# Making a positional bias by distance: a first layer over 304 to 576 columns, results read out of PSUM forwards and backwards, rows stored in a skewed raster

## The chip, the cores and the metric

The kernel runs on one core of a Trainium2 chip. The metric is the device time of one execution in microseconds; the time of a kernel is the median of several runs.

## The reference

Attention with a positional bias, followed by two feed-forward stages. The bias is what the change is about:

```
B, H, S, D = 2, 8, 576, 64          # hidden = 32
scores = scale * q @ k^T
rel = pos[:, None] - pos[None, :]
x = log1p(|rel|) / log1p(max(pos_i, 1))          # S x S
h = relu(x * w1 + b1)                            # S x S x 32
bias = h @ w2                                    # S x S x 8, one plane per head
attn = softmax(scores + bias);  out = attn @ v
# then: a mixture of 4 experts (512 -> 1024 -> 512) on 1152 tokens,
# then: a layer 512 -> 2048 -> 512 with a rational function between
```

In a row i the first factor of x depends on the column only by the distance |i - j|; the second is one number for the row.

## The kernel before

**The bias phase.** The 576 rows of the bias are made in 36 groups (`gg`) of 16 rows. Multiplied by the row's log, the hidden layer needs no division: h * psi_i = relu(w1 * log1p(|rel|) + b1 * psi_i). The partitions hold 4 rows x 32 hidden units. `hidden(gg)` makes four tiles of 128 x 576, each an addition of a per-partition shift and a maximum with zero (VectorE) or a Relu with a bias (ScalarE), out of the table `ltab` (1,148 columns: log distances, moved by one column from each of the four rows to the next, so that a window of 576 columns at the right place is what four rows need). `HIDDEN` names the engine of each: three on VectorE ("D"), one on ScalarE ("A"). `products(gg)` multiplies them on TensorE by `wm` (the second layer of the hidden network for 4 rows x 8 heads) into a pair of PSUM banks, half of the columns to a bank; three such pairs rotate. `combine(gg)` evacuates them on ScalarE, times one over the row's log, into the tile `bo`; a tile holds four groups, and two of them rotate (tag `we` of `wpool`, which the expert weights use later). After each fourth group `store` writes the tile to scratch in DRAM (`bias_d`, one tensor per 128 rows), and `load_bias` brings back 128 rows for two heads at a time, with rows on the partitions. The last 64 rows go straight from `bo` into place (`last_bias`) as well.

**Order.** Instructions run on each engine in the order in which they are written. Groups overlap: hidden rows run `LEAD` = 2 groups ahead of the products, evacuations one group behind them; hidden rows have room for four groups. SyncE's queue carries nearly all DMAs, in order: loads of q, k and v, eight small loads of constants (`setup_const`, at group 3), the stores, the loads of the bias, and the swapped copy of k (`swap_k`). Meanwhile GpSimd splits q, k and v into a high and a low part, and TensorE transposes the first of them (`qk_T`). At groups 34 and 35 the first two score groups of the attention are put in (`scores`, `biased` on VectorE, `exps` on ScalarE).

**The attention** follows in an order that a planner (`Flow`) writes out from fixed costs and due times, among them `BIAS4`, the time at which the last band of the bias is taken to be in place. It needs the stacks of q and k, the swapped k, and the bias of its rows, in groups of 128 rows and one head. Then come the expert stage and the last stage, which keep TensorE busy; the diff touches of them only the size of one tile.

Of the kernel before, what the change touches and what calls it, by code (L numbers as in the profile page):

```python
# [9 lines left out]
F32 = mybir.dt.float32  # L10
# [14 lines left out]
P = 128  # L25
# [12 lines left out]
W_MAX = f32_of_bits(0x47EFFFFF - (48 << 23))  # L38


NTQ, NDT = S // 4, 1148
LEAD = 2
START = dict(PE=0.0, ACT=2.1, DVE=2.7, POOL=3.6, SP=5.5)
BIAS4 = 7.6
EARLY_SPLIT = {22: 'k'}
EARLY = {34: (0,), 35: (1,)}
HIDDEN = ["DDDA"] * (S // 16)
OUT_DVE = ()

LAG = {"PE": .2, "ACT": .16, "DVE": .17, "POOL": .14, "SP": 2.2, "": 0.0, "own": .1, "ownPE": 0.0}  # L50
CFG = dict(S=(-46.52, 288.45, 1.92, 183.94), R=(52.57, 7.45, 22.77, 52.37),
# [83 lines left out]
class Kernel:  # L135
# [16 lines left out]
    def run(self):  # L152
# [3 lines left out]
        self.wpool = ctx.enter_context(self.pool("wpool"))  # L156
        self.stacks = ctx.enter_context(self.pool("stacks"))
        self.dram = ctx.enter_context(self.pool("dscr", DRAM))
        self.bias_d = [self.dram.tile([P, H, S] if c < 4 else [16, H, 4, S], F32, name=f"bias_d{c}") for c in range(5)]
        self.nc.scalar.preload_act_table_set("natural_log_exp_and_others")  # L160
        self.ident = self.const.tile([P, P], F32, name="ident")
        self.w_tiles = {}
# [125 lines left out]
    def load_parts(self, i, key, a, b, stg, defer):  # L288
        nc = self.nc
        if key == ("d", 0):  # L290
            hi, lo = (self.up.tile([P, a, b], F32R, tag="w64", bufs=2, name="wd" + x) for x in "hl")
        elif len(key) == 2 or (i - 2 * NPAIR + 1) % 10 < 2:
            w = self.wpool.tile([P, 4 * S], F32R, tag="we", bufs=2, name="we")
            hi, lo = (w[:, o:o + a * b].rearrange("p (a b) -> p a b", a=a) for o in (0, a * b))
        else:
            hi, lo = (self.wmoe.tile([P, a, b], F32R, tag="wm" + x, bufs=8, name="wm" + x) for x in "hl")
        nc.scalar.activation(out=hi, in_=stg, func=AF.Copy)  # L297
        self.w_tiles[key] = (hi, lo)

        def low():  # L300
            for k in range(0, a, a // 2):
                sl = slice(k, k + a // 2)
                nc.gpsimd.tensor_tensor(out=lo[:, sl], in0=stg[:, sl], in1=hi[:, sl].bitcast(F32), op=ALU.subtract)  # L303
            self.stage_w()
        defer(low)
# [65 lines left out]

    def bias_phase(self):
        nc, t, pa = self.nc, self.t, self.pa
        cw = pa.tile([P, 10], F32, name="cw")
        mask = pa.tile([P, 4], F32, name="mask")
        shift = pa.tile([P, NTQ], F32, name="shift")
        rpsi = pa.tile([P, S // 16], F32, name="rpsi")
        ltab = pa.tile([P, NDT], F32, name="ltab")  # L380
        nc.sync.dma_start(out=cw, in_=t["w1_b1_w2"])
        nc.scalar.dma_start(out=shift, in_=t["c_psi"])
        for i, (a, b) in enumerate(((NDT - 640, NDT), (0, NDT - 640))):
            nc.sync.dma_start(out=ltab[:, a:b], in_=t["c_ltab"][:, a:b])
            if i:
                nc.scalar.dma_start(out=rpsi, in_=t["c_rpsi"])
            else:
                nc.scalar.dma_start(out=mask, in_=t["c_mask"])
                nc.scalar.dma_start(out=self.ident, in_=t["c_ident"])
# [1 line left out]
            self.load_raw(0, nm)  # L391
        w1, b1 = cw[:, 0:1], cw[:, 1:2]
        nc.vector.tensor_scalar(out=shift, in0=shift, scalar1=b1, scalar2=None, op0=ALU.mult)
        nc.vector.tensor_scalar(out=ltab[:, NDT - 640:NDT], in0=ltab[:, NDT - 640:NDT], scalar1=w1, scalar2=None, op0=ALU.mult)
        wm = pa.tile([P, 4, H], F32, name="wm")
        nc.gpsimd.tensor_tensor(out=wm, in0=cw[:, 2:10].unsqueeze(1).to_broadcast([P, 4, H]),
                                in1=mask.unsqueeze(2).to_broadcast([P, 4, H]), op=ALU.mult)
        wm = wm.rearrange("p g h -> p (g h)")

        NG = S // 16  # L400
        hid, outs, banks = {}, {}, {}
        hids = self.xpool.tile([P, 16, S], F32, tag="xa", bufs=1, name="hid")

        def hidden(gg):
            for q in range(4):
                if q % 2 == 0:
                    slot = (2 * gg + q // 2) % 8
                ht = hid[gg, q] = hids[:, 2 * slot + q % 2]
                tt = 4 * gg + q
                d, c = ltab[:, 572 - 4 * tt:572 - 4 * tt + S], shift[:, tt:tt + 1]  # L410
                e = HIDDEN[gg][q]
                if e == "A":
                    nc.scalar.activation(out=ht, in_=d, func=AF.Relu, bias=c)  # L413
                else:
                    eng = nc.vector if e == "D" else nc.gpsimd
                    eng.tensor_scalar(out=ht, in0=d, scalar1=c, scalar2=0.0, op0=ALU.add, op1=ALU.max)  # L416


        def products(gg):
            ps = banks[gg] = self.ps.tile([P, 2, 512], F32, tag="ab", bufs=3, name="ps_ab")  # L420
            hs = [hid.pop((gg, q)) for q in range(4)]
            for i in range(2):
                for q in range(4):
                    nc.tensor.matmul(ps[32 * q:32 * q + 32, i, 0:288], lhsT=wm, rhs=hs[q][:, 288 * i:288 * i + 288], start=True, stop=True)  # L424

        def store(b):
            if b < 8:
                d = self.bias_d[b // 2][64 * (b % 2):64 * (b % 2) + 64].rearrange("(a q) h j -> (q h) a j", a=4)
            else:
                d = self.bias_d[4].rearrange("q h a j -> (q h) a j")  # L430
            nc.sync.dma_start(out=d, in_=outs[b])

        def combine(gg):
            b, G = divmod(gg, 4)
            if G == 0:
                outs[b] = self.wpool.tile([P, 4, S], F32, tag="we", bufs=2, name="bo")
            bo, ps = outs[b][:, G].rearrange("p (a b) -> p a b", a=2), banks.pop(gg)[:, :, 0:288]
            c = rpsi[:, gg:gg + 1]
            if gg in OUT_DVE:
                nc.vector.tensor_scalar(out=bo, in0=ps, scalar1=c, scalar2=None, op0=ALU.mult)  # L440
            else:
                nc.scalar.activation(out=bo, in_=ps, func=AF.Copy, scale=c)  # L442
            if G == 3:
                if b == 8:
                    self.bias_t[0, 4] = self.last_bias(outs[b].rearrange("(q h) a j -> h q a j", h=H))
                    self.last_band = lambda: store(b)
                else:
                    store(b)

        for gg in range(LEAD):  # L450
            hidden(gg)
        nc.vector.tensor_scalar(out=ltab[:, 0:NDT - 640], in0=ltab[:, 0:NDT - 640], scalar1=w1, scalar2=None, op0=ALU.mult)
        for nm in "kqv":
            self.split(0, nm)
            self.load_raw(1, nm)
# [25 lines left out]
                    self.swap_k(0)  # L481


    def last_bias(self, d):

        nc = self.nc
# [5 lines left out]
    def load_bias(self, p, c):  # L492
        d = self.bias_d[c]
        if c < 4:
            bt = self.front.tile([P, 2, S], F32, tag=f"bias{c}", bufs=1, name="bias")
            self.nc.sync.dma_start(out=bt, in_=d[:, 2 * p:2 * p + 2])
        else:
            bt = self.last_bias(d[:, 2 * p:2 * p + 2].rearrange("q h a j -> h q a j"))
        self.bias_t[p, c] = bt
# [745 lines left out]
def shape_consts():  # L1245
# [2 lines left out]
    Pp = np.log1p(np.maximum(d, np.float32(1.0)))  # L1248
    g = np.repeat(np.arange(4), 32)
    m = np.arange(NDT)  # L1250
    ltab = L[np.minimum(np.abs(m[None, :] - 572 - g[:, None]), S - 1)]
    r = 4 * np.repeat(np.arange(4), 32) + np.tile(np.repeat(np.arange(4), H), 4)
    rpsi = np.float32(1.0) / Pp[16 * np.arange(S // 16)[None, :] + r[:, None]]
# [2 lines left out]
        "c_mask": 8.0 * (g[:, None] == np.arange(4)[None, :]).astype(np.float32),  # L1256
        "c_psi": np.ascontiguousarray(Pp[4 * np.arange(NTQ)[None, :] + g[:, None]]),
        "c_rpsi": np.ascontiguousarray(rpsi),
        "c_ltab": np.ascontiguousarray(ltab),
    }  # L1260

# [22 lines left out]
```

## Time and profile before

| | |
|---|---|
| median of 3 runs | 808.4 us (808.29 to 808.88) |
| profiled execution: its time | 807.95 us |
| its span, first to last instruction | 806.0 us |
| TensorE / VectorE / ScalarE / GpSimd busy in the span | 97% / 81% / 61% / 56% |
| granted clock of TensorE | 0.999 |

The profile is of one execution. A row of a timeline has the start, the time until the last end, the engine and line, and what was written from what, merged over instructions of the same kind that follow each other; in square brackets stands idle time before it and what ended it. In rows that group instructions, busy time and mean duration stand behind the count, then the idle time in front of them. SPq is the queue of SyncE. PE is TensorE, DVE VectorE, ACT ScalarE, POOL GpSimd.

### The profile page before, as it was taken

To read this page: it belongs to the slowest core of one execution; us is meant where nothing else is said; L and a number is where in the kernel's file an instruction comes from. 1 tells how busy PE (TensorE), PEld (TensorE's weight loads), DVE (VectorE), ACT (ScalarE), POOL (GpSimd) and SP (SyncE) were. 2 spreads that over 40 slices of the span, in tenths; PEclk is the share of its full clock that TensorE was granted. 3 is DMA by queue.
4 is the path that set the end of the run, shared out by engine and by line. 5 is a ranking of instruction groups with operands and counts; after the bars stand their busy time and mean duration, and the time that the engine had idled before them with its cause. 6 is when DMAs were issued, how large, how long until landed. Compare 5 with 4: busy or idle time off the path is not lost.

```text
span 806.0 us, 13644 instructions
## 1 busy us (share of the span) xinstructions
PE 783.1 (97%) x4980; PEld 683.0 (85%) x4980; DVE 649.4 (81%) x1183; ACT 488.3 (61%) x932; POOL 455.0 (56%) x454
## 2 busy tenths in 40 slices
PE   6888999999999999999999999999999999999997
PEld 2337899988998999999999999999889889998986
DVE  7987888888687888878889878888678667888775
ACT  5898898889443334333333433333369998887772
POOL 3167689778346555444355545345166977754442
PEclk9999999999999999999999999999999999999999
DMA  5788747491013434432444333333130311000012
GB/s 127 264 284 229 196 104 201 105 233 54 1 30 102 131 131 129 137 116 93 147 139 144 131 105 119 117 131 105 40 105 27 119 64 53 1 0 1 1 40 78
DMA packets 67634, 87.37 MB, mean 108 GB/s; under 512 B 33520, under 2 KB 42096, under 8 KB 67440
## 3 DMA queue, kind: packets, MB, share of 16 engines
q1 hardware_dynamic: 66992, 86.35, 35.4%
q8 instruction: 39, 0.64, 0.3%
q14 instruction: 27, 0.22, 0.1%
q10 hardware_dynamic: 576, 0.16, 0.1%
HBM read 60.12 MB, written 21.36 MB: 101 GB/s over the span
## 4 chain that ended last, share of the span: by engine, by line
PE 77%; ACT 7%; POOL 6%; issue 4%; DVE 4%; DMA 2%; SPq 0%; POOLq 0%; DVEq 0%; ACTq 0%
PE ps_o L900 20%; PE ps_o L1150 11%; PE ps_y L992 10%; PE ps_h L1142 10%; PE ps_x L992 8%; PE ps L701 6%; PE ps L594 5%; PE ps L653 4%; ACT hid L413 2%; ACT bo L442 2%; POOL we L303 2%; PE ps_x L890 1%; PE ps L548 1%; POOL wml L303 1%; PE ps_y L890 1%
## 5 line engine op out<-in xcount | busy, mean ns | idle before, releaser
L900 PE MATMUL ps_o<-we,hs 128*128 128x512 f32 x810 | 203.4, 392 | 0.0
L900 PEld LDWEIGHTS ps_o<-we,hs 128*128 128x128 f32 x810 | 146.1, 188 | 25.8
L303 POOL TENSOR_TENSOR we<-wstg,we 128x512 fp32r<-128x512 f32 x40 | 57.0, 1446 | 130.3 <-ACT we L297 130.3
L906 DVE SCALAR_TENSOR_TENSOR acc<-ps_o,prob,acc 128x512 f32<-128x512 f32 x135 | 99.7, 743 | 30.1 <-PE ps_o L900 29.9
L1123 POOL TENSOR_TENSOR qq<-qq,ha 128x384 f32<-128x384 f32 x48 | 48.9, 1019 | 71.0 <-ACT qq L1120 71.0
L1150 PE MATMUL ps_o<-wmh,hs 128*128 128x512 f32 x252 | 83.5, 392 | 1.1 <-POOL hs L1134 1.1
L1142 PE MATMUL ps_h<-x,wmh 128*128 128x384 f32 x288 | 73.7, 337 | 0.0
L636 POOL TENSOR_SCALAR P<-P,ri 128x576 f32<-128x576 f32 x72 | 53.0, 747 | 33.3 <-DVE ri L627 18.8
L930 ACT ACTIVATE hs<-ps_x 128x576 fp32r<-128x576 f32 x32 | 20.8, 651 | 80.7 <-DVE ps_x L1004 74.0
L608 DVE CUSTOM_DVE_ANT_0 P<-ps,bias 128x576 f32<-128x576 f32 x72 | 53.6, 750 | 14.9 <-PE ps L594 12.9
L424 PE MATMUL ps_ab<-hid,wm 128*32 128x288 f32 x576 | 47.0, 425 | 12.0 <-DVE hid L416 7.5
L616 ACT ACTIVATE P<-P,nm 128x576 f32<-128x576 f32 x72 | 56.0, 780 | 3.3 <-DVE nm L608 3.1
L1129 DVE SCALAR_TENSOR_TENSOR qq<-qq,rr 128x384 f32<-128x384 f32 x48 | 26.6, 554 | 38.1 <-ACT rr L1128 35.1
L1150 PEld LDWEIGHTS ps_o<-wmh,hs 128*128 128x128 f32 x252 | 47.3, 188 | 11.4 <-POOL hs L1134 1.9
L328 POOL TENSOR_TENSOR wu<-wt,wu 128x512 fp32r<-128x512 f32 x28 | 36.2, 1314 | 36.4 <-ACT wu L324 36.4
L1142 PEld LDWEIGHTS ps_h<-x,wmh 128*128 128x128 f32 x288 | 52.6, 188 | 2.0
L682 DVE TENSOR_TENSOR ptl<-ps,pth 128x512 fp32r<-128x512 f32 x72 | 48.5, 683 | 5.2 <-ACT pth L678 4.7
L416 DVE TENSOR_SCALAR hid<-ltab,shift 128x576 f32<-128x576 f32 x108 | 52.6, 558 | 0.0
L594 PE MATMUL ps<-kh,qs 128*128 128x288 f32 x168 | 50.3, 321 | 1.4 <-DVE nm L608 1.3
L1134 POOL TENSOR_TENSOR hs<-pp,hs 128x384 fp32r<-128x384 f32 x48 | 48.9, 1019 | 3.5 <-issue 2.8
L424 PEld LDWEIGHTS ps_ab<-hid,wm 128*32 128x32 f32 x576 | 18.4, 112 | 37.0 <-ACT bo L442 13.9
L1150 PE MATMUL ps_o<-wml,hs 128*128 128x512 f32 x126 | 49.5, 393 | 0.0
(142 smaller groups left out, 2098.9 us busy)
## 6 DMA issues: line engine op xcount, KB each, us to landing
wstg<-moe_w SPq DMA_DIRECT2D x32, 512.0 KB, 3.7
bias_d<-bo SPq DMA_DIRECT2D x9, 1152.0 KB, 5.4
bias<-bias_d SPq DMA_DIRECT2D x16, 576.0 KB, 5.1
w<-moe_w_in SPq DMA_DIRECT2D x16, 512.0 KB, 4.4
w<-moe_w_out SPq DMA_DIRECT2D x16, 512.0 KB, 3.8
kl<-kh SPq DMA_DIRECT2D x16, 288.0 KB, 4.4
w_u<-wmag SPq DMA_DIRECT2D x16, 256.0 KB, 2.4
w_d<-wmag SPq DMA_DIRECT2D x16, 256.0 KB, 2.4
```

Source lines behind the costliest of these rows:

```text
L303: nc.gpsimd.tensor_tensor(out=lo[:, sl], in0=stg[:, sl], in1=hi[:, sl].bitcast(F32), op=ALU.subtract)
L416: eng.tensor_scalar(out=ht, in0=d, scalar1=c, scalar2=0.0, op0=ALU.add, op1=ALU.max)
L424: nc.tensor.matmul(ps[32 * q:32 * q + 32, i, 0:288], lhsT=wm, rhs=hs[q][:, 288 * i:288 * i + 288], start=True, stop=True)
L594: nc.tensor.matmul(ps[:, half, dst:dst + w], lhsT=lhs, rhs=k[:, src:src + w], start=(i == 0), stop=(i == len(m) - 1))
L608: nc.vector.tensor_tensor_reduce(out=Pt[u][:, S * h:S * h + S].rearrange("p (a b) -> p a b", a=2), in0=ps[:, :, 0:288], in1=self.bias_t[n ...
L616: nc.scalar.activation(out=pt, in_=pt, func=AF.Exp, scale=-1.0, bias=stat.pop(g), accum_out=sums[n, c][:, h:h + 1])
L636: nc.gpsimd.tensor_scalar(out=pt[:, sl], in0=pt[:, sl], scalar1=ri, scalar2=1.0, op0=ALU.mult, op1=ALU.mult)
L900: nc.tensor.matmul(ps, lhsT=a, rhs=w[:, f, :], start=(f == i == 0), stop=(f == 1 and i == 2))
L906: nc.vector.scalar_tensor_tensor(out=acc[:, t], in0=ps, scalar=pr, in1=acc[:, t], op0=ALU.mult, op1=ALU.add)
L992: nc.tensor.matmul(ps[:, half, 0:288], lhsT=wu[:, w, i, k], rhs=x[v][:, k, 288 * half:288 * half + 288], start=(start and k == j == 0), st ...
L1142: nc.tensor.matmul(ps, lhsT=w[:, k, fo:fo + P], rhs=v[:, k, :], start=(k == i == 0), stop=(k == 3 and i == 2))
L1150: nc.tensor.matmul(ps, lhsT=a[:, P * tt:P * tt + P], rhs=w[:, f % 2, :], start=(f == i == 0), stop=(f == 3 and i == 2))
```

## The change

The first 32 groups no longer make all 576 columns of their rows. They make the hidden layer once for each distance that occurs in the group, from 0 to the largest: 576 - 16 gg or 16 gg + 16 columns, whichever is more (304 to 576). The table for it, `dtab`, has 576 columns. The last four groups work as before, from the 640 columns of `ltab` that they need. A product of up to 512 columns is one matmul per tile and lies in one bank. `combine` reads it twice on ScalarE: once backwards, for the columns left of the diagonal, and once forwards; both write into one row of 591 columns. That row is the same raster for all rows of the group, though each row should be shifted by one column against the next; the shift is made in DRAM, where rows are stored at a pitch of 608 elements, and groups 16 elements closer, so that `load_bias` can read row q one element earlier than its pitch says. A tile of evacuated rows now holds two groups, and each group is stored by itself. The last four groups go into place in twelve loads instead of three. Of each three groups, two have all four hidden tiles on VectorE and one has three.

```diff
-NTQ, NDT = S // 4, 1148
+NTQ, NDT = S // 4, 640
+ROW = 608
+MARGIN = 15
...
-HIDDEN = ["DDDA"] * (S // 16)
-OUT_DVE = ()
+HIDDEN = ["DDDD", "DDDD", "DDDA"] * (S // 48)
...
-        self.bias_d = [self.dram.tile([P, H, S] if c < 4 else [16, H, 4, S], F32, name=f"bias_d{c}") for c in range(5)]
+        self.bias_d = [self.dram.tile([P + 1, H * ROW] if c < 4 else [16, H, 4, S], F32, name=f"bias_d{c}") for c in range(5)]
...
-            w = self.wpool.tile([P, 4 * S], F32R, tag="we", bufs=2, name="we")
+            w = self.wpool.tile([P, 2048], F32R, tag="we", bufs=2, name="we")
...
+        dtab = pa.tile([P, S], F32, name="dtab")
...
-        for i, (a, b) in enumerate(((NDT - 640, NDT), (0, NDT - 640))):
-            nc.sync.dma_start(out=ltab[:, a:b], in_=t["c_ltab"][:, a:b])
+        for i, (tab, nm) in enumerate(((dtab, "c_dtab"), (ltab, "c_ltab"))):
+            nc.sync.dma_start(out=tab, in_=t[nm])
...
-        nc.vector.tensor_scalar(out=ltab[:, NDT - 640:NDT], in0=ltab[:, NDT - 640:NDT], scalar1=w1, scalar2=None, op0=ALU.mult)
+        nc.vector.tensor_scalar(out=dtab, in0=dtab, scalar1=w1, scalar2=None, op0=ALU.mult)
...
+        NM = 32
...
+        def width(gg):
+            return max(S - 16 * gg, 16 * gg + 16) if gg < NM else S
...
-                ht = hid[gg, q] = hids[:, 2 * slot + q % 2]
+                ht = hid[gg, q] = hids[:, 2 * slot + q % 2, 0:width(gg)]
...
-                d, c = ltab[:, 572 - 4 * tt:572 - 4 * tt + S], shift[:, tt:tt + 1]
+                d, c = dtab[:, 0:width(gg)] if gg < NM else ltab[:, 572 - 4 * tt:572 - 4 * tt + S], shift[:, tt:tt + 1]
...
+            W = width(gg)
+            for i, (a, b) in enumerate(((0, min(W, 512)), (512, W)) if gg < NM else ((0, 288), (288, W))):
+                if b > a:
+                    for q in range(4):
+                        nc.tensor.matmul(ps[32 * q:32 * q + 32, i, 0:b - a], lhsT=wm, rhs=hs[q][:, a:b], start=True, stop=True)
+
+        def store(gg):
+
+            b, G = divmod(gg, 2)
+            o = (P * ROW - 16) * (gg % 8)
+            d = self.bias_d[gg // 8].rearrange("q x -> (q x)")[o:o + P * ROW].rearrange("(p r) -> p r", r=ROW)
+            nc.sync.dma_start(out=d[:, 0:S + MARGIN], in_=outs[b][:, G])
+
+        def store_last():
             for i in range(2):
-                for q in range(4):
-                    nc.tensor.matmul(ps[32 * q:32 * q + 32, i, 0:288], lhsT=wm, rhs=hs[q][:, 288 * i:288 * i + 288], start=True, stop=True)
-
-        def store(b):
...
+                nc.sync.dma_start(out=self.bias_d[4].rearrange("q h a j -> (q h) a j")[:, 2 * i:2 * i + 2], in_=outs[16 + i])
 
         def combine(gg):
-            b, G = divmod(gg, 4)
+            b, G = divmod(gg, 2)
+            c = rpsi[:, gg:gg + 1]
+            if gg < NM:
+                if G == 0:
+                    outs[b] = self.wpool.tile([P, 2, S + MARGIN], F32, tag="we", bufs=2, name="bo")
+                ps = banks.pop(gg).rearrange("p a s -> p (a s)")
+                m = 16 * gg + MARGIN
+                nc.scalar.activation(out=outs[b][:, G, 0:m], in_=ps[:, 1:m + 1][:, ::-1], func=AF.Copy, scale=c)
+                nc.scalar.activation(out=outs[b][:, G, m:], in_=ps[:, 0:S - 16 * gg], func=AF.Copy, scale=c)
+                store(gg)
+                return
             if G == 0:
-                outs[b] = self.wpool.tile([P, 4, S], F32, tag="we", bufs=2, name="bo")
+                outs[b] = self.wpool.tile([P, 2, S], F32, tag="we", bufs=2, name="bo")
...
+            if gg == NG - 1:
+                self.last_bias_tile()
+                for i in range(2):
+                    self.last_bias_part(self.bias_t[0, 4], outs[16 + i].rearrange("(q h) a j -> h q a j", h=H), i)
+                self.last_band = store_last
...
-        nc.vector.tensor_scalar(out=ltab[:, 0:NDT - 640], in0=ltab[:, 0:NDT - 640], scalar1=w1, scalar2=None, op0=ALU.mult)
+        nc.vector.tensor_scalar(out=ltab, in0=ltab, scalar1=w1, scalar2=None, op0=ALU.mult)
...
+    def last_bias_part(self, bt, d, i):
+
+        for k in range(2):
+            a, b = (slice(64 * h + 2 * i + k, 64 * h + 64, 4) for h in range(2))
+            for out, src in ((bt[a, 0], d[0, :, k]), (bt[b, 0, 0:512], d[1, :, k, 64:S]), (bt[b, 0, 512:S], d[1, :, k, 0:64])):
+                self.nc.sync.dma_start(out=out, in_=src)
...
-            self.nc.sync.dma_start(out=bt, in_=d[:, 2 * p:2 * p + 2])
+            o = MARGIN + 2 * p * ROW
+            d = d.rearrange("q x -> (q x)")[o:o + P * (H * ROW - 1)].rearrange("(q x) -> q x", q=P)[:, 0:2 * ROW]
+            self.nc.sync.dma_start(out=bt, in_=d.rearrange("q (h r) -> q h r", h=2)[:, :, 0:S])
```

## Rows read from the trace of the kernel before

**Rows 1.** Windows: busy time of each engine, granted clock, DMA share, GB/s.
```profile
45.00:50.00 5.00, 4.38 (x65) 1.69 (x55) 5.00 (x13) 5.00 (x9) 5.00 (x1) 1.00 0.98 333
100.00:110.00 10.00, 9.99 (x79) 9.06 (x77) 9.09 (x27) 9.16 (x23) 8.97 (x13) 1.00 0.53 120
```

**Rows 2.** Forms of instructions, first 66 us.
```profile
L416 DVE TENSOR_SCALAR hid<-ltab,shift 128x576 f32<-128x576 f32 x108 | 52.6, 558 | 0.0
...
L413 ACT ACTIVATE hid<-ltab,shift 128x576 f32<-128x576 f32 x36 | 29.3, 822 | 2.9 <-DVE ltab L394 2.9
L442 ACT ACTIVATE bo<-ps_ab,rpsi 128x576 f32<-128x576 f32 x36 | 28.3, 792 | 7.0 <-PE ps_ab L424 4.3 <-DMA bias_d<-bo 2.6
```

**Rows 3.** Timeline of VectorE, first 30 us.
```profile
4.96 2.67 DVE L416 TENSOR_SCALAR hid<-ltab,shift 128x576 f32<-128x576 f32 x6
...
8.35 9.93 DVE L416 TENSOR_SCALAR hid<-ltab,shift 128x576 f32<-128x576 f32 x13
...
18.20 9.95 DVE L416 TENSOR_SCALAR hid<-ltab,shift 128x576 f32<-128x576 f32 x23
```

**Rows 4.** Timeline of GpSimd: the last split in the early stretch.
```profile
13.03 1.48 POOL L532 TENSOR_TENSOR splv<-rawv,splv 128x576 fp32r<-128x576 f32 x1
```

**Rows 5.** Timeline of all engines, end of the bias phase.
```profile
55.73 2.65 DVE L416 TENSOR_SCALAR hid<-ltab,shift 128x576 f32<-128x576 f32 x6
...
57.35 2.47 PE L424 MATMUL ps_ab<-hid,wm 128*32 128x288 f32 x32 [0.50 <-ACT bo L442]
...
60.47 1.18 PE L424 MATMUL ps_ab<-hid,wm 128*32 128x288 f32 x16
60.58 0.76 DVE L608 CUSTOM_DVE_ANT_0 P<-ps,bias 128x576 f32<-128x576 f32 x1 [2.20 <-PE ps L594]
...
63.99 0.72 ACT L442 ACTIVATE bo<-ps_ab,rpsi 128x576 f32<-128x576 f32 x1
...
64.73 1.85 SPq L489 DMA_DIRECT2D bias<-bo  x3
```

**Rows 6.** Timeline of ScalarE, 33 to 36 us.
```profile
33.26 0.51 ACT L556 ACTIVATE kh<-ps 128x384 fp32r<-128x384 f32 x1
33.63 0.80 ACT L413 ACTIVATE hid<-ltab,shift 128x576 f32<-128x576 f32 x1
34.30 0.77 ACT L442 ACTIVATE bo<-ps_ab,rpsi 128x576 f32<-128x576 f32 x1
34.92 0.81 ACT L413 ACTIVATE hid<-ltab,shift 128x576 f32<-128x576 f32 x1
```

**Rows 7.** Waits from 15 to 62 us: total, times, longest.
```profile
ACT bo L442 <- DMA bias_d<-bo: 2.6, 1, 2.6
```

**Rows 8.** Forms of instructions, whole span.
```profile
L622 DVE TENSOR_SCALAR sm<-sm 128x1 f32<-128x1 f32 x72 | 8.3, 145 | 1.8 <-ACT P L616 1.4
...
L678 ACT ACTIVATE pth<-ps 128x512 fp32r<-128x512 f32 x72 | 41.4, 604 | 4.1 <-PE ps L653 3.5
...
L678 ACT ACTIVATE peh<-ps 128x256 fp32r<-128x256 f32 x16 | 6.3, 394 | 0.0
```

**Rows 9.** Tile wmag: duration in ns, least, median, most; first and last start.
```profile
L361 DVE TENSOR_SCALAR wmag<-wmag x32: 408/418/1400, 259.6 to 562.9; 128x512 uint32<-128x512 uint32 x32
```

**Rows 10.** Timeline of all engines, 67 to 75 us.
```profile
67.77 0.60 SPq L562 DMA_DIRECT2D kl<-kh  x1
...
70.33 0.20 DVE L622 TENSOR_SCALAR sm<-sm 128x1 f32<-128x1 f32 x2
...
74.53 0.38 PE L594 MATMUL ps<-kh,qs 128*128 128x288 f32 x1
```

**Rows 11.** The page's DMA issues: count, KB each, us from issue to landing.
```profile
bias_d<-bo SPq DMA_DIRECT2D x9, 1152.0 KB, 5.4
...
kl<-kh SPq DMA_DIRECT2D x16, 288.0 KB, 4.4
w_u<-wmag SPq DMA_DIRECT2D x16, 256.0 KB, 2.4
```

More of the change, by code (lines that the diff above doesn't have):

```diff
@@ L421, in products @@
             hs = [hid.pop((gg, q)) for q in range(4)]
-            for i in range(2):
-                for q in range(4):
-                    nc.tensor.matmul(ps[32 * q:32 * q + 32, i, 0:288], lhsT=wm, rhs=hs[q][:, 288 * i:288 * i + 288], start=True, stop=True)
-        def store(b):
[L427 to L431, printed above, removed]
@@ L435, in combine @@
             if G == 0:
-                outs[b] = self.wpool.tile([P, 4, S], F32, tag="we", bufs=2, name="bo")
+                outs[b] = self.wpool.tile([P, 2, S], F32, tag="we", bufs=2, name="bo")
             bo, ps = outs[b][:, G].rearrange("p (a b) -> p a b", a=2), banks.pop(gg)[:, :, 0:288]
[L438 to L448, printed above, removed]
+            nc.scalar.activation(out=bo, in_=ps, func=AF.Copy, scale=c)
+            if gg == NG - 1:
[3 more added lines that the diff above has]
+                self.last_band = store_last
@@ L481, in bias_phase, with last_bias_tile @@
                     self.swap_k(0)
+    def last_bias_tile(self):
+        self.bias_t[0, 4] = self.front.tile([P, 2, S], F32, tag="bias4", bufs=1, name="bias")
+    def last_bias_part(self, bt, d, i):
[3 more added lines that the diff above has]
+                self.nc.sync.dma_start(out=out, in_=src)
     def last_bias(self, d):
@@ L1250, in shape_consts @@
     m = np.arange(NDT)
+    dtab = np.broadcast_to(L[None, :], (P, S))
     ltab = L[np.minimum(np.abs(m[None, :] - 572 - g[:, None]), S - 1)]
@@ L1258, in shape_consts @@
         "c_rpsi": np.ascontiguousarray(rpsi),
+        "c_dtab": np.ascontiguousarray(dtab),
         "c_ltab": np.ascontiguousarray(ltab),
```

## The prediction

> **What bounds the kernel now.** I first cut the span into windows and compared the stretch in which the bias is made with a later one. In the later stretch TensorE is busy all the time. In the bias stretch TensorE has holes, while VectorE, ScalarE and the 16 DMA engines all stand at or near full [rows 1]. So what happens there is decided by a race of three, and the rest of the kernel merely starts when the race is over. The forms of the instructions name the racers: 108 hidden rows on VectorE, 36 hidden rows and 36 evacuations on ScalarE [rows 2].
>
> The VectorE timeline tells more than "busy". Twenty-three hidden rows on end from 18.20 take 9.95: 0.43 us each. From 8.35, 13 of them need 9.93 instead of 5.6 [rows 3], while GpSimd works on its splits until 14.5 [rows 4]. 108 x 0.43 = 46.4 of the 53.4 us between 4.96 and 58.38; scaling, small instructions and the time lost beside GpSimd make up the rest. VectorE never waits: it sets its own end at 58.38 (55.73 + 2.65) [rows 5].
>
> ScalarE runs at the same pace: from start to start 0.62 for an evacuation and 0.67 for a hidden row [rows 6], 1.29 a group against 3 x 0.43 = 1.29. But it was thrown back once by 2.6 us, waiting for a store to free its buffer [rows 7], and so it is behind when VectorE is done: TensorE then waits for its banks, the first attention scores come late, and VectorE sits idle for 2.20 us before its first `biased` at 60.58. From there to the end of the last evacuation (63.99 + 0.72 = 64.71) run 4.13 us of fixed order [rows 5]. The attention starts from that.
>
> **The change, term by term.** A group is 16 rows of the bias; its width w is now the larger of 576 - 16g and 16g + 16 for the first 32 groups, and 576 for the last four. Summed over the 36 groups that is 15,936 columns instead of 20,736. But VectorE takes 132 of the 144 hidden rows instead of 108: 58,416 columns instead of 62,208.
>
> *VectorE.* What matters is how much of the 0.43 is fixed. An instruction on one column lasts 0.145 [rows 8], one on 512 columns 0.408 at the least [rows 9]: (0.408 - 0.145)/511 = 0.52 ns a column, so 576 columns are 0.30 and the fixed share is 0.13. Bounds: two one-column instructions together took 0.20, so the second added only 0.055 [rows 10]; and the whole 0.145. The sum with 0.13 is 132 x 0.13 + 58,416 x 0.00052 = 47.5, that is 1.1 above 46.4. With a fixed share of 0.055 (0.65 ns a column) it is 45.2, 1.2 below; with 0.145, 48.1, 1.7 above. I take +1.1, since rate and fixed share then agree with both durations. Two tables are scaled as before, of 576 and 640 columns and not 640 and 508: +68 columns, 0.04, and the first is loaded sooner by as little; I leave both out. VectorE ends at 58.38 + 1.1 = 59.5 (57.2 to 60.1). The time lost beside GpSimd stays: the same six split instructions, at the same place.
>
> *ScalarE.* Two thirds of its hidden rows go, 24 of 36; those left are 5,328 columns in 12 instructions. Each evacuation becomes two, over 591 columns. Copies out of PSUM of 512 and 256 columns last 0.604 and 0.394, 0.82 ns a column [rows 8]; an evacuation of 576 takes 0.62 until the next instruction starts [rows 6], so 0.15 is fixed. Two parts: 2 x 0.15 + 591 x 0.00082 = 0.79. A group costs ScalarE 0.79 + about 0.19 for a third of a hidden row (0.55 for the 444 columns that it has on average) + 0.1 for the copies of q and k (nine of 0.37 [rows 6]): 1.08, below VectorE's 47.5/36 = 1.32. No row shows a read with a negative step. Lower bound: as forwards. Upper bound: twice as long, 8,416 reversed columns x 0.82 = 6.9 us. I take the lower, because the elements that are read lie side by side, as they do in the nearest rows.
>
> The Trainium skill (ScalarE: Activation LUTs, What ACT_TABLE_LOAD costs) gives an ACTIVATE with one per-partition operand about 280 ns + 0.833 ns a column, with 93 ns of overlap; by this estimate the two parts take 0.87 and not 0.79, ScalarE is still not the bound and the sum is unchanged, but the loop of the next paragraph becomes 0.04 longer a group.
>
> *The new wait.* A buffer of evacuated rows holds two groups and not four, and there are still two of them. So the evacuation of group 2b waits until the store of group 2b - 3 has landed. A store is now 128 x 2,364 B = 295 KB. By the issues, 256 KB land in 2.4 and 1,152 KB in 5.4 [rows 11]; on that line 295 KB take 2.5, and I take 2.7 since loads of the bias cross it. In a turn of four groups there are this landing, handoffs of 0.2, two evacuations (1.6), two thirds of a hidden row and half a copy (0.55): 5.05, or 1.26 a group. VectorE needs 1.46 a group for groups 0 to 8, 1.18 for 9 to 26, 1.47 for the last nine. So ScalarE falls behind by 18 x 0.08 = 1.4 in the middle and gets it back at the end. VectorE does not feel a lag below some 4 us: three PSUM banks and four groups of hidden rows lie between them. Behind ScalarE's wait are TensorE's products alone. SyncE now issues 32 stores, which must not queue behind each other's landing: their destinations don't overlap. I count 0 here; without the cover it is the rival below.
>
> The Trainium skill (DMA: Bandwidth & Descriptors, Measured) asks for transfers of 1 MiB and more, since each DMA pays about 2 us whatever its size; its fit gives 2.7 for one of these stores. By this rule the loop decides only if the landing grows well beyond that.
>
> *TensorE.* 1.18 a group [rows 5] falls with the width, to 0.91 on average: hidden behind VectorE.
>
> *The end.* ScalarE is no longer late, so products 34 run while VectorE makes the last three hidden rows (1.29): 1.18, then the four score matmuls (from 59.82, when the products before them end, to 60.47: 0.65) and the handoff (0.11) [rows 5]. `biased` comes about 0.75 after VectorE's last hidden row, not 2.20: -1.45.
>
> *Behind the bias.* The last band goes into place in twelve loads instead of three. Three took 1.85 [rows 5], 0.62 each; six of the twelve need only groups 32 and 33 and go early, six come after the last evacuation, 3.7 instead of 1.85. Everything behind them on SyncE moves 1.85 back: the swapped k, issued at 67.77 and used by the tenth scores at 74.53 [rows 10], lands in about 4.4 [rows 11], a margin of 2.3. The raw loads behind have no margin that I can prove; I count +0.2 (0 to 1.9).
>
> *Sum:* +1.1 - 1.45 + 0 + 0.2 = -0.15, and +0.3 for a little lag that is not made up: 807.95 + 0.15 = 808.1 for an execution like the profiled one, whose span of 806.0 has 1.95 around it. The median of the runs lies 0.45 above the profiled one, so 808.6. A change below 0.2% (1.6 us) is about what a measurement of this kernel can't tell from none.
>
> **Rivals.** *The store loop decides* (slower). For it: the DMA engines are at 0.98 in the bias stretch [rows 1] and ScalarE has waited for a store before [rows 7]. Against: 295 KB are a quarter of what is queued there now. Beyond 1.42 a group (a landing of 3.35) the last nine groups no longer make good the lag. At 3.5 a group takes 1.46: 18 x 0.28 = 5.0 behind after the middle, of which nothing is made up until the last four groups, which store nothing; about 4 reach the end: 808.6 - 0.3 + 4 = 812.3. Chance 0.23.
>
> *The reversed read is slow* (slower): 0.22 more a group, which makes the loop 1.47 and ends as above, 812; worse if it costs more than twice. Against: nothing in the rows, for: nothing either. Chance 0.08.
>
> *VectorE's fixed share is small* (faster): with 0.055 VectorE ends at 57.2, 1.2 before its old end, and with the 1.45 of the end and 0.2 behind it the total is -2.45: 806.0. For it: the pair of one-column instructions [rows 10]. Against: those are not streams of hundreds of columns. Chance 0.27, a saving from the narrower products that I may have missed included.
>
> *My forecast*, VectorE decides and gains and losses cancel: 807 to 810, chance 0.42.
>
> **How the numbers follow.** Faster by over 0.2%: 0.27. Within: 0.42. Slower: 0.23 + 0.08 = 0.31. The range takes in the fast rival and the slow ones at the landing of 3.5: 805.6 to 812.5, with about 0.08 below and 0.12 above.
>
> **What would show it.** Right: VectorE without idle time up to about 59.5; a hidden row of 304 columns every 0.29; evacuations in two parts of together about 0.79; ScalarE with idle time that ends with PE, not with a DMA; `biased` within a microsecond of the last hidden row. Wrong: ScalarE's waits on bias_d stores sum to several microseconds, or a reversed part lasts longer than a forward one of its width, or SyncE's stores start only when the one before has landed, which would make each group over 2.5 us and the forecast worthless; or a hole in TensorE around the ninth and tenth score groups, from the twelve loads.

## The result, and the profile after

The changed kernel takes 814.83 us (median of 4 runs, 814.36 to 816.64) against 808.64 for the kernel before on the same chip: a ratio of 1.0082, 95% interval 1.0070 to 1.0094. It is slower, by 6 us, and above the range forecast. The execution whose trace follows took 814.37, with a span of 812.6 (before: 806.0) and a mean granted clock of 0.991.

The windows of the changed kernel, to be held against [rows 1]: busy time of TensorE, its weight loads, VectorE, ScalarE and GpSimd, granted clock, DMA share, GB/s.

```profile
40.00:45.00 5.00, 4.64 (x35) 1.16 (x35) 3.64 (x10) 5.00 (x13) 2.29 (x3) 0.66 0.70 208
45.00:50.00 5.00, 1.56 (x18) 0.32 (x16) 4.97 (x14) 1.71 (x5) 0.00 (x0) 1.00 0.90 249
50.00:55.00 5.00, 3.79 (x23) 0.99 (x27) 2.87 (x7) 2.82 (x7) 0.00 (x0) 0.57 0.71 274
```

The race of three is gone. From 45 to 50 ScalarE works 1.71 of 5 us where it worked all 5; from 50 to 55 VectorE, the engine that was to set the end, works 2.87. The waits from 5 to 75 us, in total, times, and the longest, show who holds them up (compare [rows 7], one wait of 2.6):

```profile
DVE hid L426 <- PE ps_ab L436: 4.9, 4, 1.5
...
ACT bo L457 <- DMA bias_d<-bo: 9.5, 4, 3.3
...
ACT bo L464 <- DMA bias_d<-bo: 2.3, 2, 2.0
```

ScalarE stands 11.8 us before evacuations whose row buffer is still being stored. Behind it TensorE has no free bank, and behind that VectorE has no free rows to write: the last link costs it 4.9 us. How long a store takes to land, from the tile view of `bias_d` from 28 to 68 us, stores and loads together (in the issue view the 22 stores from 30 to 64 us have a median of 4.1 as well):

```profile
DMA to landing us min/median/max: 2.1/4.1/6.4
```

One more wait for a store hides under another name. The evacuation at 24.75 stood for 2.96 us; the view of the waits puts that down to TensorE, whose products for it had ended at about 22.1. It starts 0.1 after a store has landed, as the four of the list do. That store took only 2.4 us, but it was issued at 22.29, 3.4 us after its evacuation had ended, because the eight small loads of constants (from 17.71 on) stand ahead of it in SyncE's queue. VectorE does not wait behind this one.

The holes that the waits leave in TensorE also bring its clock down, to 0.50 from 41 to 43 and from 51 to 57 us (windows of 1 us). The products of two groups then take 3.01 us instead of 1.54:

```profile
45.02 1.54 PE L436 MATMUL ps_ab<-hid,wm 128*32 128x384 f32 x16
50.26 3.01 PE L436 MATMUL ps_ab<-hid,wm 128*32 128x416 f32 x16 [3.69 <-ACT bo L458]
```

VectorE waits for these products, so a part of its 4.9 us is the clock's; no run separates it from the wait that causes it.

The end of the bias phase on the timeline, to be held against [rows 5]:

```profile
58.01 6.10 DVE L426 TENSOR_SCALAR hid<-ltab,shift 128x576 f32<-128x576 f32 x14
...
64.80 0.76 DVE L641 CUSTOM_DVE_ANT_0 P<-ps,bias 128x576 f32<-128x576 f32 x1 [0.69 <-PE ps L627]
...
67.44 0.74 ACT L464 ACTIVATE bo<-ps_ab,rpsi 128x576 f32<-128x576 f32 x1 [0.32 <-DMA bias_d<-bo]
67.73 0.76 DVE L641 CUSTOM_DVE_ANT_0 P<-ps,bias 128x576 f32<-128x576 f32 x1 [2.16 <-PE ps L627]
67.83 7.49 SPq L513 DMA_DIRECT2D bias<-bo  x12
...
69.31 0.72 ACT L464 ACTIVATE bo<-ps_ab,rpsi 128x576 f32<-128x576 f32 x1
```

VectorE ends its hidden rows at 64.11 (58.01 + 6.10), 5.7 later than before. The first `biased` follows 0.69 later, the second only after 2.93, because ScalarE waits twice more for stores. The last evacuation ends at 70.03 (69.31 + 0.72), 5.3 later than before.

The remaining 1.2 to 1.3 us of the span's 6.6 arise behind it. TensorE idles 2.18 us until the last evacuations free its banks, and then its clock falls:

```profile
70.08 0.71 PE L581 MATMUL ps<-identr,splk 128*128 128x128 f32 x6 [2.18 <-ACT bo L464]
...
71.49 0.44 PE L627 MATMUL ps<-kl,qs 128*128 128x288 f32 x1
71.73 0.44 PE L627 MATMUL ps<-kh,qs 128*128 128x288 f32 x1
```

```profile
72.00:73.00 1.00, 1.00 (x7) 0.98 (x6) 0.81 (x3) 0.71 (x2) 1.00 (x3) 0.50 0.15 41
73.00:74.00 1.00, 1.00 (x6) 1.00 (x5) 0.21 (x2) 0.78 (x4) 1.00 (x1) 0.50 0.12 33
```

Score matmuls start 0.24 apart instead of 0.13, at a granted clock of 0.50 (windows of 1 us), the 1.2 GHz level. The profiled execution of the kernel before has the same hole (2.17 us, until 64.76) and keeps clock 1.00 from 62 to 66. So the account, against that execution, is 5.3 to the last evacuation and about 1.2 behind it.

That execution, with a mean clock of 0.999, is not typical in this. Of the 48 executions of the kernel before that were timed beside the experiments, 17 show 0.999, with a median span of 805.7, and 31 show 0.997 or 0.998, with one of 806.9. So a fall of the clock that costs about 1.2 us seems to come and go in the kernel before as well (a mean does not say where it fell). The changed kernel shows 0.991 to 0.993 in all four.

### The profile page after: what moved, and what is told of

Same layout as the page of the kernel before. It is cut to its first block, busy times and chain, and to the rows that moved or that the text cites. A ratio compares the mean times of both kernels' runs of the same rounds, so it can differ in the third digit from the quotient of the medians.

```text
span 812.6 us, 13235 instructions
## 1 busy us (share of the span) xinstructions
PE 781.5 (96%) x4756; PEld 678.5 (84%) x4756; DVE 649.9 (80%) x1207; ACT 477.5 (59%) x940; POOL 445.6 (55%) x454
## 4 chain that ended last, share of the span: by engine, by line
PE 77%; DVE 5%; POOL 5%; ACT 5%; issue 4%; DMA 3%; SPq 0%; ACTq 0%; POOLq 0%; DVEq 0%
PE ps_o L933 20%; PE ps_y L1025 10%; PE ps_o L1183 10%; PE ps_h L1175 9%; PE ps_x L1025 8%; PE ps L734 6%; PE ps L627 5%; PE ps L686 4%; DMA bias_d<-bo 2%; DVE hid L426 2%; POOL we L304 2%; POOL wml L304 1%; PE ps L581 1%; PE ps_x L923 1%; PE ps_ab L436 1%
## 5 line engine op out<-in xcount | busy, mean ns | idle before, releaser
L436 PE MATMUL ps_ab<-hid,wm 128*32 128x288 f32 (+18 forms) x352 | 43.8, 542 | 20.2 <-ACT bo L458 11.2
L436 PEld LDWEIGHTS ps_ab<-hid,wm 128*32 128x32 f32 x352 | 12.5, 115 | 46.4 <-ACT bo L458 24.6
L426 DVE TENSOR_SCALAR hid<-dtab,shift 128x512 f32<-128x512 f32 (+17 forms) x118 | 46.3, 465 | 5.0 <-PE ps_ab L436 4.9
```

What stands on the lines that cost most here:

```text
L436: nc.tensor.matmul(ps[32 * q:32 * q + 32, i, 0:b - a], lhsT=wm, rhs=hs[q][:, a:b], start=True, stop=True)
```

## The experiments

Theory A: the row buffers hold half as many groups, so ScalarE waits for stores to land. The rivals: the twelve loads at the end, the skew or the small size of the transfers as such, the reversed read, the loads of the bias that cross the stores, and the clock. All medians are of timed rounds, each ratio to the kernel before on the same chip.

### Four pairs of row buffers

```diff
-outs[b] = self.wpool.tile([P, 2, S + MARGIN], F32, tag="we", bufs=2, name="bo")
+outs[b] = pa.tile([P, 2, S + MARGIN], F32, tag="bo", bufs=4, name="bo")
```

(A pair is a tile `bo` of two groups. The last four groups keep the two tiles of tag `we` for themselves here, so they no longer wait for stores of earlier groups either.)

> The changed kernel with four instead of two rotating buffers of evacuated rows (two groups each); nothing else differs. Theory A, the store loop: ScalarE stood 11.8 us in six waits for stores to land, and VectorE 4.9 us idle behind it; with four buffers a store has six groups of time to land, so both sums fall below 1 us, VectorE ends its hidden rows near 59.5 us as forecast (64.1 in the changed kernel), TensorE's granted clock stays at 1.00 in the bias stretch, and the time is 807.5 to 809.5 us. Theory B, the transfers: rows of 2,364 B and loads shifted by single elements make the DMA engines the bound; buffers then only postpone the wait, ScalarE still waits 5 us or more on stores, and the time stays above 812 us. Theory C, the clock: less work per group lets the granted clock fall by itself; it then falls here too, and the time is 810 to 813 us.

Measured: 807.28 us, ratio 0.9991 (0.9981 to 1.0000). The waits, the timeline and the windows:

```profile
ACT bo L457 <- DMA bias_d<-bo: 0.9, 1, 0.9
```

```profile
36.50 21.94 POOL L560 TENSOR_SCALAR splk<-rawk 128x576 fp32r<-128x576 f32 x1 [4.02 <-PE ps L581]
...
51.81 6.10 DVE L426 TENSOR_SCALAR hid<-ltab,shift 128x576 f32<-128x576 f32 x14
58.60 0.76 DVE L641 CUSTOM_DVE_ANT_0 P<-ps,bias 128x576 f32<-128x576 f32 x1 [0.69 <-PE ps L627]
...
62.01 0.72 ACT L464 ACTIVATE bo<-ps_ab,rpsi 128x576 f32<-128x576 f32 x1
```

```profile
30.00:40.00 10.00, 10.00 (x80) 4.57 (x78) 10.00 (x36) 9.60 (x24) 3.77 (x2) 1.00 0.97 315
40.00:50.00 10.00, 10.00 (x71) 4.09 (x69) 10.00 (x29) 7.92 (x19) 10.00 (x1) 1.00 0.98 315
...
60.00:70.00 10.00, 7.43 (x47) 6.95 (x46) 5.74 (x18) 7.71 (x18) 5.63 (x8) 0.83 0.38 104
```

All else of the change is kept, and the loss is gone: 0.0091 of the ratio, 7.4 us. The issue view gives these stores a median landing of 4.8 between 20 and 68 us, against 3.8 in the changed kernel: they land later, since they now follow one another without pauses (DMA share 0.97 to 0.98 from 30 to 50), and nobody waits. So the harm is neither the size of a store nor its slowness as such, but that two pairs of buffers leave no time for it. Theory C falls with theory B: without the wait the clock stays at 1.00 from 20 to 60 us. VectorE ends its hidden rows at 57.91, 0.5 before the old end, and the last evacuation ends 2.0 earlier (62.73 against 64.71). The span is only 0.8 shorter: the clock falls behind the hole here too, to 0.83 in the window from 60 to 70.

### The same, and the last band in three loads

```diff
-for i in range(2):
-    self.last_bias_part(self.bias_t[0, 4], outs[16 + i].rearrange("(q h) a j -> h q a j", h=H), i)
+self.bias_t[0, 4] = self.last_bias(outs[8].rearrange("(q h) a j -> h q a j", h=H))
```

> The same with the last four groups in one tile again, put in place by three loads instead of twelve. If the twelve loads cost something behind the bias (SyncE reached the swapped k 5.4 us after the last evacuation, before 1.9), this is 0.5 to 1.5 us faster than four buffers alone; if they are hidden, the same within 0.5 us.

Measured: 807.02 us, ratio 0.9989 (0.9980 to 0.9999). The twelve loads cost too little to see beside the interval: their issues, 7.49 us long in the changed kernel, delay nothing that shows in the time.

### The kernel before with halved buffers

```diff
-outs[b] = self.wpool.tile([P, 4, S], F32, tag="we", bufs=2, name="bo")
+outs[b] = self.wpool.tile([P, 2, S], F32, tag="we", bufs=2, name="bo")
```

(with the group count per buffer, the stores of 576 KB and the twelve loads to match)

> The kernel before with buffers of two groups instead of four (stores of 576 KB, twelve loads of the last band): the halved buffers alone. Theory A: a turn of four groups takes a landing of about 3.5, two evacuations and two hidden rows of ScalarE, 0.2 of handoffs: 1.5 to 1.6 a group instead of 1.29, so 8 to 11 us slower than before, 816 to 819 us, with ScalarE waiting for stores in every second group. Theory B: rows of 2,304 B, not skewed, land in time: 808 to 811 us.

Measured: 816.51 us, ratio 1.0109 (1.0093 to 1.0124). Its waits:

```profile
ACT bo L443 <- DMA bias_d<-bo: 9.6, 8, 3.5
```

The halved buffers alone, without the narrow products, the reversed reads or the skew, do at least the harm of the whole change: 8.5 us. (The twelve loads are in it too, which cost nothing visible above, and its stores are twice as large.) So theory A is shown from both sides: the wait taken away takes the loss away, and halved buffers alone bring it. ScalarE waits eight times, not in every second group as expected; the longest wait, 3.48 at 25.71, is again for a store issued behind the eight small loads.

### The loads of the bias moved behind the stores

```diff
-if gg % 8 == 4 and 4 < gg < NG or gg == NG - 1:
-    self.load_bias(0, gg // 8 - 1)
+if gg >= 32 and gg < NG:
+    self.load_bias(0, gg - 32)
```

> The changed kernel with the first three loads of the bias moved from groups 12, 20 and 28 to groups 32, 33 and 34. Stores issued near these loads took 4.6 to 6.4 us to land, others 2.1 to 4.1. If it is the loads crossing the stores that opens the loop, the three longest waits of ScalarE (2.7, 3.3 and 2.0 us) fall below 1 us and the time to 809 to 811.5 us, or 1 to 2 more if the first scores now wait for their bias. If the stores delay each other, the waits stay and the time is 814 to 817 us.

Measured: 812.63 us, ratio 1.0066 (1.0049 to 1.0083). The interval overlaps that of the changed kernel, so the gain in time alone is not clear of noise; the trace shows what changed. Waits, issues from 20 to 68 us, and timelines:

```profile
ACT bo L457 <- DMA bias_d<-bo: 7.2, 3, 3.4
```

```profile
bias_d<-bo SPq DMA_DIRECT2D x29, 295.5 KB, 2.5
```

```profile
25.05 0.35 ACT L457 ACTIVATE bo<-ps_ab,rpsi 128x111 f32<-128x111 f32 x1 [3.38 <-DMA bias_d<-bo]
```

```profile
53.55 6.09 DVE L426 TENSOR_SCALAR hid<-ltab,shift 128x576 f32<-128x576 f32 x14
63.15 0.76 DVE L641 CUSTOM_DVE_ANT_0 P<-ps,bias 128x576 f32<-128x576 f32 x1 [3.51 <-DMA bias<-bias_d]
```

The expectation was met in part: the time lies in its wider band, but two waits of over 3 us stay that should have gone. Without loads that cross them the stores land in a median of 2.5 instead of 3.8, VectorE waits once for 0.52 and ends its hidden rows at 59.64, close to the 59.5 of the forecast. So crossing transfers are what makes the landing long. Of the waits that are left (3.38 at 25.05, 0.53 at 38.62 and 3.30 at 46.09) the last agrees: the stores issued from 39 to 42, behind two transfers of the swapped k, have a median of 5.7, those from 52 to 56 one of 2.1. The first has another cause: its store landed in 2.8 but was issued late, at 22.12, behind the eight small loads. And the first `biased` now waits 3.51 us for its own load, so that most of the gain is given back at once.

### The skew

```diff
-o = (P * ROW - 16) * (gg % 8)
+o = P * ROW * (gg % 8)
...
-o = MARGIN + 2 * p * ROW
-d = d.rearrange("q x -> (q x)")[o:o + P * (H * ROW - 1)].rearrange("(q x) -> q x", q=P)[:, 0:2 * ROW]
+o = 2 * p * ROW
+d = d.rearrange("q x -> (q x)")[0:P * H * ROW].rearrange("(q x) -> q x", q=P)[:, o:o + 2 * ROW]
```

(in the version with four pairs of buffers)

> The version with four pairs of row buffers, but the rows are stored and read back in a straight raster: each group's rows start 16 x 608 words further on, and each partition of a load starts a whole line of eight rows after the one before, not a word earlier (the bias is then shifted wrongly, so the output is not the reference's). If the skew costs the transfers nothing: 807.3, as with the skew, store landing 4 to 4.5. If rows that start off the 64-byte grid make stores or loads slow: landing below 3.5 and DMA share below 0.95 from 30 to 50, and 806.5 or less.

Measured: 807.12 us, ratio 0.9979 (0.9970 to 0.9989). The issues from 20 to 68 us, with KB each and the median landing, of this version:

```profile
bias_d<-bo SPq DMA_DIRECT2D x29, 295.5 KB, 4.8
bias<-bias_d SPq DMA_DIRECT2D x4, 576.0 KB, 4.8
```

With the skew the same lines read 4.8 and 4.7. The skew costs the transfers nothing that shows; the two ratios differ by 0.0012 with intervals that overlap, so up to some 2 us stay open.

### Products added in TensorE's hole

```diff
+if gg == NG:
+    ps = self.ps.tile([P, 2, 512], F32, tag="ab", bufs=3, name="ps_fill")
+    for r in range(2):
+        for i in range(2):
+            for q in range(4):
+                nc.tensor.matmul(ps[32 * q:32 * q + 32, i, 0:288], lhsT=wm, rhs=hids[:, 12 + q, 288 * i:288 * i + 288], start=True, stop=True)
```

(in the version with four pairs of buffers and three loads; the products are extra work that nobody reads)

> Four buffers and three loads of the last band, and in TensorE's hole of 2.2 us between the bias and the attention two more rounds of the last group's products (16 matmuls by the program, written to a spare bank and read by nobody: work added, no result changed). In the kernel without them the granted clock stands at 0.50 from 64.0 to about 67.8 us, after the hole; in the kernel before the same hole is not followed by a drop. Theory: it is the drop that eats the 1.2 us between what the bias phase gains (last evacuation 2.0 to 2.9 us earlier than before) and what the time gains (0.9). Then the clock stays at 1.00, and this is 1.0 to 1.5 us faster than without, 805.5 to 806.3 us. Rival: SyncE's later loads or GpSimd cost it; the clock is repaired or not, and the time stays within 0.4 us of the kernel without.

Measured: 805.88 us, ratio 0.9972 (0.9961 to 0.9983). TensorE's timeline, then the window that follows the hole, first with the added products and then without them:

```profile
60.24 2.15 PE L486 MATMUL ps_fill<-hid,wm 128*32 128x288 f32 x32
62.57 0.93 PE L584 MATMUL ps<-identr,splk 128*128 128x128 f32 x9 [0.18 <-PE ps_fill L486]
```

```profile
64.00:66.00 2.00, 2.00 (x15) 1.74 (x14) 1.65 (x5) 1.35 (x4) 2.00 (x4) 1.00 0.72 169
```

```profile
64.00:66.00 2.00, 2.00 (x12) 1.99 (x11) 1.37 (x4) 1.28 (x3) 2.00 (x3) 0.53 0.68 159
```

The hole shrinks from 2.17 to 0.18 us, the clock stays at 1.00, and the ratio is 0.0017 lower, 1.4 us; the two intervals overlap by 0.0003, and the spans differ by 1.0 (804.0 against 805.0). That agrees with the 1.2 that the account above gives to the clock. All seven executions show a mean clock of 0.999 or 1.000, with a median span of 804.1; of the thirty of the versions with four pairs and no added products, eight do, with 804.4, and 22 show less, with 805.3. So the products bring nothing beyond an execution whose clock did not fall; they made each of the seven such a one.

### The same products in the changed kernel itself

> The changed kernel itself with the added products in the hole, nothing else. The clock's drop after the bias (0.50 from 71.5 to 74.5 us) is then the only thing repaired: 1.0 to 1.5 us faster than the changed kernel, 813.3 to 813.9 us, by the theory that its loss of 6.2 us is 5 us of the store loop and 1.2 us of the clock; the same within 0.4 us if the clock costs nothing.

Measured: 815.57 us, ratio 1.0096 (1.0076 to 1.0116): no gain, and a missed expectation. The windows show why:

```profile
66.00:68.00 2.00, 1.74 (x17) 0.60 (x18) 0.00 (x0) 1.91 (x5) 0.00 (x0) 0.71 0.04 13
68.00:70.00 2.00, 2.00 (x12) 1.21 (x16) 0.80 (x3) 0.43 (x2) 0.00 (x0) 0.50 0.59 112
```

Here a wait for a store makes an earlier hole, from 64.3 to 66.3; the clock falls behind that one, and the added products themselves begin at 0.50 and take 2.69 us instead of 2.15. The last evacuation ends at 71.49, later than without them (70.03). While the store wait makes holes, filling one of them moves the fall and does not take it away.

### Hidden rows moved from VectorE to ScalarE

```diff
-HIDDEN = ["DDDD", "DDDD", "DDDA"] * (S // 48)
+HIDDEN = ["DDAA"] * 6 + ["DDDA"] * 3 + ["DDDD", "DDDD", "DDDA"] * 6 + ["DDDA", "DDDD", "DDDA", "DDDD", "DDDA"] + ["DDDA"] * 4
```

(with six pairs of buffers and three loads; 28 hidden rows on ScalarE instead of 12, so the count in the text below is wrong)

> Four-buffer kernel with six buffers, three loads, and 50 hidden tiles on ScalarE instead of 12 moved there where it stands idle: two of four in the first six groups, one of four in most of the wide ones. VectorE is the bound by theory A once the buffers don't wait: its sum of hidden rows falls by about 5 us (fewer rows in the contended stretch before 15 us above all), so it ends near 53 us. If VectorE is the only bound: 803 to 805 us. If the DMA engines are the next one (0.97 busy between 30 and 50 us with four buffers; 32 stores of 0.3 MB and four loads of 0.6 MB from 15 us on at about 0.32 MB a us end at about 53 to 55 us), the gain is 1 to 2.5 us: 804.5 to 806.

Measured: 800.54 us, ratio 0.9904 (0.9889 to 0.9919), better than either band expected, so neither had the size right.

```profile
46.06 5.23 DVE L426 TENSOR_SCALAR hid<-ltab,shift 128x576 f32<-128x576 f32 x12
51.98 0.76 DVE L638 CUSTOM_DVE_ANT_0 P<-ps,bias 128x576 f32<-128x576 f32 x1 [0.70 <-PE ps L624]
...
55.39 0.72 ACT L463 ACTIVATE bo<-ps_ab,rpsi 128x576 f32<-128x576 f32 x1
```

ScalarE now waits for no store up to 75 us and has room, and VectorE ends at 51.29, 7.1 before the old kernel. The last evacuation ends 8.6 earlier (56.11) and the span is 7.5 shorter; the clock falls to 0.51 from 56 to 58, the likely taker of the other 1.1. This version beats both kernels. The sixth pair of buffers and the moved rows came in together, and no run moves the rows with two pairs. With the added products as well:

> The rebalanced kernel with the same added products in the hole. If the clock's drop is there as well, 1.0 to 1.5 us faster than the rebalanced kernel; if the denser last groups (three rows of each on VectorE, as before the change) already prevent it, the same within 0.4 us.

Measured: 800.3 us, ratio 0.9898 (0.9880 to 0.9916). The clock is 1.000, the time is the same, so the 1.0 to 1.5 us expected are missed. What the clock gives is lost, in the profiled execution, to a transfer of the swapped k that is next in line, on TensorE's timeline (without the products this matmul runs at 67.36 and does not wait):

```profile
67.78 0.37 PE L630 MATMUL ps<-kl,qs 128*128 128x288 f32 x1 [0.82 <-DMA kl<-kh]
```

### The moved rows in the kernel before

```diff
-HIDDEN = ["DDDA"] * (S // 16)
+HIDDEN = ["DDAA"] * 6 + ["DDDA"] * 30
```

> The kernel before with one edit: in the first six groups two of the four hidden rows go to ScalarE, not one (102 hidden rows on VectorE, 42 on ScalarE). Theory A (the gain of the version with moved hidden rows needs the room that the change makes on ScalarE): the old ScalarE already spends 1.29 a group, as much as VectorE, so six more rows of 0.67 put it 4.0 further behind, VectorE saves 6 x 0.43 = 2.6 at most and then waits behind it: 808 to 811. Theory B (VectorE's slow start beside GpSimd is simply relieved, and the change has no part in it): 805 to 806.

Measured: 807.73 us, ratio 0.9995 (0.9986 to 1.0004): no difference, just below theory A's band and well above theory B's. Its timeline of VectorE, and its waits from 5 to 75 us:

```profile
51.52 6.52 DVE L416 TENSOR_SCALAR hid<-ltab,shift 128x576 f32<-128x576 f32 x15
60.77 0.76 DVE L608 CUSTOM_DVE_ANT_0 P<-ps,bias 128x576 f32<-128x576 f32 x1 [2.73 <-PE ps L594]
```

```profile
ACT bo L442 <- DMA bias_d<-bo: 3.3, 1, 3.3
...
DVE hid L416 <- PE ps_ab L424: 1.6, 2, 1.4
```

Six rows fewer, and VectorE ends only 0.3 earlier (58.04); its first `biased` comes 0.2 later than before, since ScalarE is the later of the two. So theory B falls: the old kernel does not gain from the moved rows as it stands. Two things hold it, and the run does not separate them. At 25.96 VectorE is 2.2 us ahead of the kernel before (28.18 there), but ScalarE waits 3.3 us for a store to free its old buffer, and VectorE loses 1.6 behind it. From then on ScalarE works without a pause until 60.7, which is theory A's lack of room. The old kernel with more buffers, with or without moved rows, wasn't run, nor were the other ten moved rows on it; how much of the 8 us needs the narrower layer stays open.

## Why the prediction was wrong

**The step that failed is the new wait**, put as "I count 0 here". It was the right loop with the wrong landing. The step took 2.7 for a store, a line through transfers of [rows 11], with 0.2 for loads that cross it. Measured are 2.1 for a store with next to nothing beside it (the one issued at 31.3), a median of 3.8 over all the stores, and 6.3 and 6.4 for two issued beside the load at 45.77. With 3.8 the step's own turn is 6.15 us, 1.54 a group: slower than VectorE in every stretch, which is the case of its rival. The Trainium skill (DMA: Bandwidth & Descriptors, Anatomy of one DMA) gives a fixed part of about 2 us for any DMA and, by its fit, which is for transfers issued from GpSimd, an estimate of 2.7 for one of these; the store alone agrees with the order of that, the ones in traffic do not.

Two signs stood in the prediction's own rows. The 2.4 for 256 KB comes from a later stretch, where the DMA share is about 0.4; in the bias stretch it is up to 0.98 [rows 1]. And [rows 11] also has 288 KB, almost this size, landing in 4.4 (the swapped k): the prediction uses that figure further down, but not for the store. The margin was also thinner than stated. By the step's own rates the last nine groups make good the lag up to 1.28 a group (18 x 0.10 = 9 x 0.19, rounded), a landing of 2.8. At 1.42, a landing of 3.35, they give back 9 x 0.05 = 0.45 of 18 x 0.24 = 4.3.

**A mean did not do.** The step held that a lag below some 4 us isn't felt. ScalarE is not held back a little in each turn, but four times for 1.35 to 3.29 us, and this is passed on to VectorE three links further: 4.9 us, the slow clock of the products included. Its lag was also to end with the last four groups, which store nothing; instead their first buffer waits 1.99 and the second 0.32 for stores of earlier groups, which puts the second `biased` 2.93 behind the first. So the rival's 812.3 was short as well: it had 4 at the end, the trace has 5.3.

**The clock was not foreseen**: about 1.2 us behind the bias phase of the changed kernel, 1.0 to 1.4 by the run with the hole filled. Most executions of the kernel before seem to pay this too, so it is not all the change's.

**VectorE, +1.1:** its rate was right. On the timelines of the changed kernel:

```profile
31.66 0.42 ACT L457 ACTIVATE bo<-ps_ab,rpsi 128x191 f32<-128x191 f32 x1
...
32.41 7.85 DVE L426 TENSOR_SCALAR hid<-dtab,shift 128x320 f32<-128x320 f32 x26
32.44 0.45 ACT L457 ACTIVATE bo<-ps_ab,rpsi 128x207 f32<-128x207 f32 x1
...
41.81 0.54 ACT L457 ACTIVATE bo<-ps_ab,rpsi 128x303 f32<-128x303 f32 x1
42.20 0.53 ACT L458 ACTIVATE bo<-ps_ab,rpsi 128x288 f32<-128x288 f32 x1
42.59 0.57 ACT L457 ACTIVATE bo<-ps_ab,rpsi 128x319 f32<-128x319 f32 x1
```

Twenty-six rows of about 330 columns take 0.30 each and those of 576 0.43 to 0.44: at 0.52 ns a column the fixed share is again 0.13 (these two alone give 0.54 and 0.12), and the rival of a small fixed share falls. Yet with the wait removed VectorE ends at 57.91 and not at 59.5. The likely reason is GpSimd. Before, its split of k ran under the hidden rows, and where its first half ends and its second half runs, from 50.2 to 52.7, they lost time; the old timeline of GpSimd and the old window:

```profile
38.07 12.76 POOL L527 TENSOR_SCALAR splk<-rawk 128x576 fp32r<-128x576 f32 x1 [6.56 <-PE ps L548]
50.91 1.49 POOL L532 TENSOR_TENSOR splk<-rawk,splk 128x576 fp32r<-128x576 f32 x1
```

```profile
50.00:60.00 10.00, 8.78 (x121) 3.48 (x118) 8.38 (x16) 10.00 (x18) 2.41 (x3) 1.00 0.73 255
```

Sixteen rows take 8.38 there, 1.5 more than at 0.43 each. With four pairs of buffers the first half of the split lasts until 58.44, after VectorE's last row, and the second half falls behind the phase. This is read from the traces; no run moved the split alone.

**ScalarE, 0.79 for two parts:** right. Whole pairs start 0.78 apart (31.66, 32.44). The Trainium skill (ScalarE: Activation LUTs, What ACT_TABLE_LOAD costs) gave 0.87 by the prediction's estimate; the trace decides for the smaller. The reversed read costs what a forward one does: 303 columns backwards until the next start 0.39, 288 forwards 0.39. That rival falls.

**The end and behind it:** for the first `biased`, 0.75 after the last hidden row was right (0.69). For the twelve loads 0.2 was counted, and nothing larger shows.

**Net:** without the wait the change does about what the sum said, a draw: 0.9991 against a forecast of 808.6 to 808.4. That is in part luck: VectorE ends 1.6 earlier than the sum has it, and the clock, which the sum does not have, takes about 1.2 back in the profiled execution.

## What to carry to other kernels

A smaller buffer turns a transfer that nobody waited for into one that sets the pace: price its landing in the traffic that it will meet, at the worst of it and not only the mean, and count what stands ahead of it in its queue, before counting the wait at nothing. When work on a bound engine changes places with a wait, look at who has become idle: the change paid only in the run that gave it more buffers and also used the room on ScalarE (800.5 us). And a hole in TensorE can cost more than its length, so compare the clock of the stretch behind it, over more than one execution.

## What the runs showed of the hardware

- The granted clock of TensorE fell to 0.50 for some 3 us after a hole of 2.2 us in the changed kernel (71 to 74.5), with four pairs of buffers (64 to 67), and with moved rows (56 to 59), and not after an equal hole in the profiled execution of the kernel before. By the mean clocks, 31 of 48 other executions of the kernel before seem to have a fall as well, and are about 1.2 us longer. What decides it was not isolated.
- Stores of 295 KB land in 2.1 us with next to nothing beside them, in 2.5 at the median with the loads of the bias moved away, in 4.8 at the median with four pairs of buffers (DMA share 0.97 to 0.98 from 30 to 50 us), and in up to 6.4 beside a load in the changed kernel.
- A GpSimd instruction that shares time with back-to-back VectorE work can last many times longer: the first half of the split of k took 2.86 us in the changed kernel and 21.94 with four pairs of buffers, and in both it ended 0.5 us after VectorE stopped. In the kernel before it took 12.76 and ended while VectorE was still at work.
- ScalarE reads PSUM backwards at the price of forwards: 0.39 us to the next start for 303 columns backwards and for 288 forwards.
